# First expert layer with an unsplit fp32 w2: a second product in full fp32, and low halves of w1 on VectorE alone

## The chip, the cores and the metric

One core of a Trainium2 chip runs the whole program. The metric is device time of one execution in microseconds (us), of which the median of a few executions is taken. TensorE (PE) does matrix products and writes PSUM; VectorE (DVE), ScalarE (ACT) and GpSimd (POOL) do elementwise work; SyncE (SP) issues the plain transfers, GpSimd the indexed ones.

## The reference, cut to what matters

Attention comes first, with the query pooled in pairs; its output is a matrix `x` of 2304 tokens by 512. Two expert layers follow, each with eight experts of 512 x 1024 and 1024 x 512 weights. In the first, a token is computed only where its skip score is positive:

```python
for e in range(E):                       # first layer; second: the same with a further gate
    mask = e_idx == e
    h = np.maximum(xc[mask] @ w1[e], 0.0)
    y[mask] = gate_w[mask, None] * (h @ w2[e])
out[do_compute] = xc + y                 # x of the second layer
```

All data are float32.

## The kernel before

**Numbers.** TensorE takes an operand either as fp32 or as fp32r, a reduced form. A product near fp32 accuracy is built here of three fp32r products: each operand is split into a high half (a cast to fp32r) and a low half (what is left of it), and high x high, high x low and low x high are added in PSUM. So w1, w2, the tokens `x` and the hidden values `h` each have a high and a low tile (`w1h`/`w1l`, `w2h`/`w2l`, `xh`/`xl`, `hh`/`hl`).

**Weights.** Per expert, w1 and w2 come as 16 chunks of 256 KB (128 partitions x 512 values): chunks 0 to 7 are w1, 8 to 15 are w2. `load_w(s)` issues them on SP into a ring `raw` of 15 chunks; chunk c waits for the landing of chunk c - 4 (`DEPTH`) and for its ring slot, that is, for the split of the chunk that held it. `split(s, c)` makes the halves: the high one on ScalarE (line 188), the low one, a subtraction (line 190), on GpSimd for the chunks in the lists below (in most units of the first layer seven of sixteen, four of them in w1) and else on VectorE. Weight tiles exist twice, for even and odd s.

```python
POOL_P0 = (1, 3)                              # first unit of the first layer
POOL_LO = (1, 3, 5, 7, 10, 12, 14)            # its other units
POOL_L2 = (5, 7, 9, 11, 13, 15)               # second layer
```

**Units.** Tokens are listed by expert in a table, and a unit works on 256 or 128 of them with one expert's weights. Each layer begins with one unit P (256 tokens, of the fullest expert); then for each of the eight experts there is a unit F (128 tokens), and, behind branches that depend on the counts, units D (256 tokens more) and at most one S (128 tokens more). A block of 128 tokens has one second product, so P and D have two blocks, F and S one. In this data the first layer runs P, eight F (called F0 to F7 here), two D, behind F2, and one S, behind F5: 15 blocks. The order is P, F0 to F2, D, D, F3 to F5, S, F6, F7.

**Inside F and S** (`gemm1_S`, `gemm2`): 24 products of w1 (line 815), a copy of the result and its transposes (819, 824), ReLU with split (206, 207), then 24 products of w2 in two halves (834) with the transposes of the next tokens between them (198). The split of the next expert's weights (unit F and P alone) is spread over the unit, w1 within the first product, w2 after it.

**Routing for the second layer** (`route2`) rides along in each first-layer unit for the block finished before: transposes of its output (857), logits (868, 882), then a chain of small VectorE operations from line 884 to 892 that ends in `ohs`, which products on lines 901 to 905 read. Those stand in TensorE's order between the transposes on line 824 and the second product.

**Order.** Each engine runs its instructions in order; the ends of the units F are branches (lines 1068 and 1069). All of SP's loads for unit s + 2 are issued at the end of unit s. GpSimd issues the gather of the next tokens, the scatter of results and the table's records at the head of each unit.

**Around it.** The weights of P are loaded and split during the last of 16 head pairs of the attention, two chunks per step j; four of P's eight w1 groups run amid the attention's last work.

Of the kernel before, what the change touches and what calls it, by code (L numbers as in the profile page):

```python
# [25 lines left out]
F = 1024  # L26
# [10 lines left out]
BIG = 65536.0  # L37
EPS = 1e-9
DEPTH = 4
RING = 15  # L40
# [75 lines left out]
def build(ctx, tc, kT, qT, vt, wg, wa1, wa2, cst, out):  # L116
# [26 lines left out]
    ident = C("ident")  # L143

    def load_w(s):
        if s >= 18:
            return
        m, j = divmod(s, 9)
        e = j - 1 if j else nc.sync.value_load(eP[0:1, m:m + 1], min_val=0, max_val=7)
        w = (wa1, wa2)[m][ds(e, 1)].rearrange("o p (c f) -> (o p) c f", f=512)  # L150
        ins = []

        def chunk(c):
            i = nc.sync.dma_start(raw[:, (16 * s + c) % RING, :], w[:, c, :])
            if c >= DEPTH:
                tc.add_manual_dep(i.ins, ins[c - DEPTH].ins.name,
                                  mybir.DependencyInfo(mybir.DependencyClass.Sync, mybir.DependencyReason.DATA),
                                  reason="few loads in flight")
            ins.append(i)

        for c in range(RING):
            chunk(c)
        rest[s] = chunk

    def behind(i, js):
# [6 lines left out]

    def split(s, c, pool=POOL_LO, dve=(), after=()):
        if s >= 18:
            return
        i = s % 2
        r = raw[:, (16 * s + c) % RING, :]
# [12 lines left out]
        behind(eng.tensor_tensor(l, r, h.bitcast(F32), ALU.subtract), after)  # L190
        if c < 16 - RING:
            rest[s](RING + c)
# [11 lines left out]

    def relu_split(ps, hi, lo):
# [3 lines left out]
    def gemm1_D(i, post, cs_=range(8), banks=None):  # L209
        for c in cs_:  # L210
            o = (banks or pH)[c % 3][:, :256]
            cc = slice(c * P, (c + 1) * P)
            n = 0
            for k in range(4):
                for w, x in ((w1h[i], xh), (w1h[i], xl), (w1l[i], xh)):
                    nc.tensor.matmul(o, w[:, k, cc], x[:, k, :], start=(n == 0), stop=(n == 11))  # L216
                    n += 1
            relu_split(o, hh[c // 4][:, c % 4, :], hl[c // 4][:, c % 4, :])
            post(c)
# [5 lines left out]
    rest = {}  # L225
    w1h, w1l, w2h, w2l, hh, hl = ([None] * 2 for _ in range(6))
    with ExitStack() as es_:
# [402 lines left out]
        for p in range(NP):  # L630
# [8 lines left out]
            for j in range(KT):  # L639
# [65 lines left out]
                if p == NP - 1 and j == 0:  # L705
# [6 lines left out]
                    w1h[0], w1l[0] = (mp.tile([P, 4, F], F32R, name=n) for n in ("w1h0", "w1l0"))  # L712
                    w2h[0], w2l[0] = (mp.tile([P, 8, 512], F32R, name=n) for n in ("w2h0", "w2l0"))
# [3 lines left out]
                    hh[0], hl[0] = (mp.tile([P, 4, 2 * P], F32R, name=n) for n in ("hh0", "hl0"))  # L717
                    load_w(0)
                if p == NP - 1:
# [13 lines left out]
        def early_chunk(c):  # L733
            if c < NP0:
                gemm1_D(0, lambda c: None, (c,), (pH[0], pX[0], pX[1]))

# [27 lines left out]
    t72 = mp.tile([1, 8, 9], F32, name="t72")  # L764
    hh[1], hl[1] = (mp.tile([P, 4, 2 * P], F32R, name=n) for n in ("hh1", "hl1"))
    xc, yo = (mp.tile([P, 2, DM], F32, name=n) for n in ("xc", "yo"))
# [39 lines left out]

    def gemm1_S(i, hook):
        hq = (ht, xc[:, 0, :])
# [12 lines left out]
        for f in range(2):  # L821
            o = pH[2 - 2 * f]
            for k in range(4):
                nc.tensor.transpose(o[:, k * P:(k + 1) * P], hq[f][:, k * P:(k + 1) * P], ident)  # L824
            relu_split(o.rearrange("p (k c) -> p k c", c=P), hh[f][:, :, :P], hl[f][:, :, :P])
            hook(5 + f)

    def gemm2(i, o, h, fs):
# [103 lines left out]
    def unit(m, kind, e, pos, urgent=(), ahead=None):  # L932
# [36 lines left out]
        def pre(*cs):  # L969
            if kind in "FP":  # L970
                for c in cs:
                    split(s + 1, c, POOL_P0 if first else POOL_LO if not m else POOL_L2, DVE_F[m], urgent if e == 0 else ())

# [4 lines left out]
        if kind == "D":  # L978
            steps = {0: head, R2D[0]: lambda: r2(0), R2D[1]: lambda: r2(1), R2D[2]: lambda: r2(2)}
            gemm1_D(i, lambda c: steps[c]() if c in steps else None)  # L980
            gemm2(i, 0, 0, (0, 1))
            half()
            r2(3)
            xprep()
            gemm2(i, 1, 1, (0,))
            if m == 0:
                turn(0)
            if ahead:
                ahead()
            gemm2(i, 1, 1, (1,))  # L990
            return
        if kind == "P":
# [21 lines left out]
            if first:  # L1014
                head()
            gemm1_D(i, post, range(NP0 if first else 0, 8))
            pre(*range(8, PB[m]))
            gemm2(i, 0, 0, (0, 1))
            half()
            pre(*range(PB[m], 16))  # L1020
            load_w(s + 2)
            gemm2(i, 1, 1, (0,))
            if m == 0:
                turn(0)
            j = gemm2(i, 1, 1, (1,))
# [10 lines left out]

        gemm1_S(i, hook)
        j = gemm2(i, 1, 0, (0,))
# [6 lines left out]
        gemm2(i, 1, 0, (1,))  # L1045

# [5 lines left out]

    for m in range(2):
        x = unit(m, "P", -1, 0)
        codes = []
# [58 lines left out]
```

## Time and profile before

| | |
|---|---|
| median of 3 executions | 1203.73 us (1199.67 to 1214.24) |
| profiled execution, whole | 1207.56 us |
| its span, first to last instruction | 1205.9 us |
| mean granted TensorE clock | 0.948 |
| busy: PE, DVE, ACT, POOL | 1057.7, 843.0, 604.1, 432.6 us |
| attention | up to 563 us |
| first expert layer, end of P to start of the second layer | 599.46 to 860.14 us |

Busy time is the union of an engine's instructions; for PE the ends are modelled, and a PE that waits at half clock counts as busy. The profiled execution is 3.8 us above the median. What a change in the first layer does is to be read from the units between 599 and 860 us.

### The profile page before, as it was taken

The page shows a single profiled execution, that of the slowest core. Times are in us where ns is not written, and L with a number is a line of the kernel's source. Part 1 is how long each engine was busy: PE and PEld are TensorE (multiplying, and loading weights), DVE is VectorE, ACT ScalarE, POOL GpSimd, SP SyncE. Part 2 cuts the span into 40 slices and gives each one's busy share as a digit, 9 for nine tenths or more (in the row PEclk, how much of TensorE's full clock was granted, in tenths as well). Part 3 has the DMA queues.
Part 4 walks back from the last instruction along what each step waited for, and adds up shares of the span by engine and source line. Part 5 has one row for each costly group of instructions (what it writes and reads, how often), then busy time and mean ns, then how long its engine had stood idle before and what let it go on. Part 6 is the DMA issues. An engine that isn't in the chain of part 4 may idle for free. (4 is left out here: it accounts for less than half of the span.)

```text
span 1205.9 us, 19802 instructions
## 1 busy us (share of the span) xinstructions
PE 1057.7 (88%) x6520; PEld 799.7 (66%) x6520; DVE 843.0 (70%) x1486; ACT 604.1 (50%) x1466; POOL 432.6 (36%) x481
## 2 busy tenths in 40 slices
PE   3899998999999998899876997778788898989987
PEld 2666665666666666565755885566676786879865
DVE  6789998899899989875777536767955335452252
ACT  3566665666656665455564325636544326241142
POOL 6222222322121223100565325656756236451252
PEclk9899999999999999899997998989898999999989
DMA  9644443334244432053376304545757246451010
GB/s 229 161 109 109 109 109 99 92 90 100 66 109 106 102 88 60 19 176 116 119 238 197 107 30 144 179 138 170 223 171 227 62 137 205 150 195 35 22 44 21
DMA packets 72955, 146.58 MB, mean 122 GB/s; under 512 B 12652, under 2 KB 21612, under 8 KB 72738
## 3 DMA queue, kind: packets, MB, share of 16 engines
q1 hardware_dynamic: 63330, 127.65, 37.1%
q0 software_dynamic: 9408, 16.48, 4.5%
q8 instruction: 82, 1.34, 0.5%
q14 instruction: 135, 1.11, 0.3%
HBM read 138.18 MB, written 15.05 MB: 127 GB/s over the span
## 5 line engine op out<-in xcount | busy, mean ns | idle before, releaser
L385 ACT ACTIVATE PT<-pS 128x288 f32<-128x288 f32 x576 | 206.5, 409 | 143.0 <-PE pS L384 141.3
L358 DVE TENSOR_REDUCE mx<-pA 128x1 f32<-128x1152 f32 x144 | 194.9, 1356 | 27.3 <-PE pA L353 20.1
L381 PE MATMUL pS<-QQ,KK 128*128 128x288 f32 x576 | 184.6, 334 | 19.5 <-ACT PT L385 19.1
L392 PE MATMUL pO<-PT,V 128*64 128x288 f32 x1152 | 182.5, 427 | 0.0
L384 PE MATMUL pS<-QM,KB 73*128 73x288 f32 x576 | 166.5, 300 | 0.0
L338 POOL TENSOR_TENSOR QM<-qs,QQ 64x576 fp32r<-64x576 f32 x32 | 48.4, 1513 | 315.8 <-ACT QQ L324 216.0
L381 PEld LDWEIGHTS pS<-QQ,KK 128*128 128x128 f32 x576 | 110.3, 192 | 71.5 <-ACT PT L385 29.8
L207 DVE SCALAR_TENSOR_TENSOR hl<-pH,hh 128x256 fp32r<-128x256 f32 (+1 forms) x114 | 57.6, 505 | 78.7 <-ACT hh L206 78.2
L384 PEld LDWEIGHTS pS<-QM,KB 73*128 73x128 f32 x576 | 111.3, 193 | 0.0
L392 PEld LDWEIGHTS pO<-PT,V 128*64 128x64 f32 x1152 | 72.7, 138 | 55.3 <-issue 27.6
L353 PE MATMUL pA<-KK,QQ 128*128 128x384 f32 x384 | 92.8, 352 | 18.3 <-DVE KK L308 9.7
L188 ACT CAST w1h<-raw 128x512 fp32r<-128x512 f32 x141 | 79.1, 620 | 50.3 <-PEq L1074 29.4
L206 ACT ACTIVATE hh<-pH 128x256 fp32r<-128x256 f32 (+1 forms) x114 | 51.5, 452 | 93.7 <-PE pH L216 78.5
L190 DVE TENSOR_TENSOR w1l<-raw,w1h 128x512 fp32r<-128x512 f32 x94 | 83.9, 925 | 18.3 <-ACT w1h L188 18.1
L834 PE MATMUL pY<-w2h,hl 128*128 128x512 f32 x304 | 86.9, 409 | 10.9 <-DVE hl L207 10.9
L834 PE MATMUL pY<-w2h,hh 128*128 128x512 f32 x304 | 96.2, 441 | 0.0
L405 DVE TENSOR_TENSOR acc<-acc,PT 128x576 f32<-128x576 f32 x128 | 94.9, 761 | 1.0
L190 POOL TENSOR_TENSOR w2l<-raw,w2h 128x512 fp32r<-128x512 f32 x56 | 80.4, 1449 | 41.6 <-ACT w2h L188 29.6
L815 PE MATMUL pH<-w1h,xh 128*128 128x512 f32 x144 | 65.8, 457 | 28.4 <-ACT w1h L188 11.4
L216 PE MATMUL pH<-xh,w1h 128*128 128x256 f32 x312 | 89.4, 287 | 1.2 <-DVE hl L207 0.9
L834 PE MATMUL pY<-w2l,hh 128*128 128x512 f32 x304 | 89.5, 418 | 0.0
L216 PE MATMUL pH<-xl,w1h 128*128 128x256 f32 x312 | 88.2, 283 | 1.1 <-DVE xl L202 1.1
(218 smaller groups left out, 2136.3 us busy)
## 6 DMA issues: line engine op xcount, KB each, us to landing
raw<-wa SPq DMA_DIRECT2D x288, 256.0 KB, 3.7
rawQ<-qT SPq DMA_DIRECT2D x64, 288.0 KB, 6.9
rawK<-kT SPq DMA_DIRECT2D x64, 288.0 KB, 4.5
V<-vt SPq DMA_DIRECT2D x16, 576.0 KB, 5.5
xb<-xr SPq DMA_DIRECT2D x14, 288.0 KB, 2.7
xg<-xb,idn POOLq DMA_INDIRECT x54, 3.6
xb<-xr POOLq DMA_DIRECT2D x2, 288.0 KB, 3.9
tab<-rec,pidx POOLq DMA_INDIRECT x24, 2.1
```

Of the source, the lines that this page charges most:

```text
L188: behind(nc.scalar.copy(h, r), after)
L190: behind(eng.tensor_tensor(l, r, h.bitcast(F32), ALU.subtract), after)
L216: nc.tensor.matmul(o, w[:, k, cc], x[:, k, :], start=(n == 0), stop=(n == 11))
L353: nc.tensor.matmul(o, QQ[h][i][:, u * P:(u + 1) * P], KK[h][i][:, cc], start=True, stop=True)
L358: i = nc.vector.tensor_reduce(mx[p % 2 if p or t < 5 else 1][:, t:t + 1], pA[:, :, :384], AX.XY, ALU.max)
L381: m = nc.tensor.matmul(o, KK[h][i][:, k], QQ[h][i][:, c], start=True, stop=False)
L384: nc.tensor.matmul(o, KB[h][p % 2][:64 + NB, k], QM[h][i][:64 + NB, c], start=False, stop=True)
L385: exps.append(nc.scalar.activation(PT[(p * KT + j) % 4][h][:, c], o, AF.Exp, scale=0.0625))
L392: i = nc.tensor.matmul(pO[f][64 * h:64 * h + 64, :HQ], V[p % 3][:, j, h, :], PT[(p * KT + j) % 4][h][:, c], start=(j == 0), stop=(j == KT ...
L405: nc.vector.tensor_tensor(a, a, t, ALU.add)
L815: nc.tensor.matmul(pH[f], x[:, k, :P], w[:, k, fc], start=(n == 0), stop=(n == 11))
L834: j = nc.tensor.matmul(pY[o], a[:, k, hc], w[:, 4 * f + k, :], start=(n == 0), stop=(n == 23))
```

## The change

In the first layer, w2 is loaded straight into an fp32 tile `w2r` (one for even, one for odd s) and used as it is; the hidden values are one fp32 tile `hr`, written by ScalarE's ReLU; `gemm2` is 8 fp32 products per block in place of 24 fp32r ones. There is no split of w2 and no `hl`. The ring holds w1 alone, so a load of eight chunks takes 8 slots of 15. `load_w2(s + 1)` is issued at the head of unit s, `load_w(s + 2)` at its end, as before. All low halves of w1 are made on VectorE. The second layer keeps its three fp32r products and `POOL_L2`; its w2 tiles take the place of `w2r` and `hr` after the first layer. F7 splits weights of the second layer and so uses `POOL_L2` in place of `POOL_LO`.

```diff
-POOL_P0 = (1, 3)
-POOL_LO = (1, 3, 5, 7, 10, 12, 14)
+NL = 9
+    def slot(s, c):
+        return (8 * s + c if s < NL else 8 * NL + 16 * (s - NL) + c) % RING
...
-        for c in range(RING):
+        for c in range(8 if s < NL else RING):
             chunk(c)
+    def load_w2(s):
+        if s >= NL:
+            return
+        w = source(s)
+        ins = []
+        for k in range(8):
+            few(nc.sync.dma_start(w2r[s % 2][:, k, :], w[:, 8 + k, :]), ins)
...
-    def split(s, c, pool=POOL_LO, dve=(), after=()):
-        if s >= 18:
+    def split(s, c, dve=(), after=()):
+        if s >= 2 * NL or (s < NL and c >= 8):
             return
...
-        eng = nc.gpsimd if c in pool else nc.vector
+        eng = nc.gpsimd if s >= NL and c in POOL_L2 else nc.vector
...
+    def relu_split(m, ps, f, k):
+        if m == 0:
+            nc.scalar.activation(hr[f][k], ps, AF.Relu)
+            return
...
+            if m == 0:
+                for k in range(4):
+                    j = nc.tensor.matmul(pY[o], hr[f][:, k, hc], w2r[i][:, 4 * f + k, :],
+                                         start=(f + k == 0), stop=(f * k == 3))
+                continue
...
-                    for c in range(2 * j, min(2 * j + 2, 16)):
-                        split(0, c, (), DVE_HI)
+                    if j < 8:
+                        split(0, j, DVE_HI)
...
             if n == 0:
                 head()
+                if kind == "F" and m == 0:
+                    load_w2(s + 1)
...
+        if m:
+            zero.close()
+            mo = pool(ctx, "mo")
+            w2h[0], w2l[0] = (mo.tile([P, 8, 512], F32R, name=n) for n in ("w2h0", "w2l0"))
+            hl[0], hl[1] = (mo.tile([P, 4, 2 * P], F32R, name=n) for n in ("hl0", "hl1"))
```

`few` is the old rule of four loads in flight, as a function of its own; the slots of w2 loads are not part of the ring.

## Rows read from the trace of the kernel before

**Rows 1.** Windows, F0 to F7: length, busy us (instructions), PEclk, DMA share, GB/s.
```profile
599.46:621.96 22.50, 17.26 (x83) 13.29 (x82) 17.51 (x37) 13.96 (x29) 12.55 (x11) 0.87 0.88 286
621.96:646.62 24.66, 16.97 (x86) 13.18 (x86) 19.26 (x38) 13.72 (x28) 15.41 (x17) 0.85 0.68 214
646.62:670.57 23.95, 18.69 (x85) 14.67 (x86) 19.45 (x38) 12.21 (x25) 17.98 (x23) 0.80 0.58 179
670.57:696.29 25.72, 25.72 (x178) 22.89 (x177) 9.11 (x36) 7.06 (x16) 6.88 (x11) 1.00 0.16 52
...
726.83:750.96 24.13, 19.04 (x86) 14.51 (x86) 17.76 (x37) 13.50 (x28) 13.47 (x12) 0.83 0.59 175
750.96:775.64 24.68, 18.23 (x86) 14.10 (x86) 19.31 (x38) 13.59 (x27) 15.48 (x18) 0.86 0.59 186
775.64:800.06 24.42, 18.25 (x86) 13.64 (x86) 19.09 (x38) 12.15 (x25) 15.66 (x18) 0.86 0.58 177
800.06:815.23 15.17, 15.04 (x86) 11.91 (x86) 6.75 (x29) 6.46 (x13) 8.54 (x17) 1.00 0.15 51
815.23:837.51 22.28, 16.53 (x86) 12.80 (x85) 18.22 (x38) 13.28 (x27) 12.74 (x11) 0.92 0.58 177
837.51:860.14 22.63, 18.07 (x86) 13.51 (x86) 19.01 (x39) 12.34 (x26) 15.84 (x18) 0.85 0.67 210
```

**Rows 2.** Waits of PE from 599.4 to 837.6 us: total, times, longest.
```profile
PE pR L901 <- DVE ohs L892: 25.9, 6, 5.3
PE pH L815 <- DVEq L1068: 6.1, 3, 2.5
...
PE pY L834 <- DVE hl L207: 4.1, 1, 4.1
PE pH L815 <- ACT w1h L188: 3.1, 2, 1.7
PE pH L815 <- DVEq L1069: 1.9, 1, 1.9
```

**Rows 3.** Timelines of DVE and POOL, units S and F6: start, length, instruction.
```profile
805.92 0.17 DVE L887 TENSOR_TENSOR sm<-lgs,s 128x16 f32<-128x16 f32 x1
...
821.26 4.42 DVE L887 TENSOR_TENSOR sm<-lgs,s 128x16 f32<-128x16 f32 x1
...
820.67 3.75 POOL L190 TENSOR_TENSOR w1l<-raw,w1h 128x512 fp32r<-128x512 f32 x3
```

**Rows 4.** Line 190 from 599.46 to 837.51 us: ns min/median/max.
```profile
L190 DVE TENSOR_TENSOR w1l<-raw,w1h x28: 678/691/6182, 600.5 to 825.8; 128x512 fp32r<-128x512 f32 x28
```

**Rows 5.** Timeline of PE, end of unit S: fp32r products.
```profile
814.30 1.09 PE L834 MATMUL pY<-w2h,hl 128*128 128x512 f32 x4
815.23 0.40 PE L815 MATMUL pH<-w1h,xh 128*128 128x512 f32 x1
```

**Rows 6.** Timelines of PE and its weight loads: fp32 products.
```profile
300.14 1.19 PE L392 MATMUL pO<-PT,V 128*64 128x288 f32 x8
301.26 0.40 PE L381 MATMUL pS<-QQ,KK 128*128 128x288 f32 x1
...
704.02 0.64 PE L868 MATMUL pR<-x2T,wgs 128*32 128x256 f32 x8
...
706.01 0.53 PEld L882 LDWEIGHTS pR<-cs,x2T 128*128 128x128 f32 x4
```

**Rows 7.** Timeline of SP: loads of weight chunks issued one behind another.
```profile
594.11 27.33 SPq L154 DMA_DIRECT2D raw<-wa  x29
```

**Rows 8.** Timelines of DVE and PE, end of unit P.
```profile
590.54 5.30 DVE L190 TENSOR_TENSOR w2l<-raw,w2h 128x512 fp32r<-128x512 f32 x6
...
596.56 0.66 PE L857 MATMUL pX<-cs,yo 128*128 128x128 f32 x4 [2.35 <-DVE yo L841]
```

**Rows 9.** Last head pair, 530 to 563 us: casts of w2, waits of weight loads.
```profile
L188 ACT CAST w2h<-raw x7: 610/620/622, 544.8 to 555.4; 128x512 fp32r<-128x512 f32 x7
...
PEld pS L381 <- ACT PT L385: 4.8, 11, 0.4
```

More of the change, by code (lines that the diff above doesn't have):

```diff
@@ L143, in build, with source, few @@
     ident = C("ident")
+    def slot(s, c):
+        return (8 * s + c if s < NL else 8 * NL + 16 * (s - NL) + c) % RING
+    def source(s):
+        if s not in src_of:
+            m, j = divmod(s, NL)
+            e = j - 1 if j else nc.sync.value_load(eP[0:1, m:m + 1], min_val=0, max_val=7)
+            src_of[s] = (wa1, wa2)[m][ds(e, 1)].rearrange("o p (c f) -> (o p) c f", f=512)
+        return src_of[s]
+    def few(i, ins):
+        if len(ins) >= DEPTH:
+            tc.add_manual_dep(i.ins, ins[-DEPTH].ins.name,
+                              mybir.DependencyInfo(mybir.DependencyClass.Sync, mybir.DependencyReason.DATA),
+                              reason="few loads in flight")
+        ins.append(i)
     def load_w(s):
-        if s >= 18:
+        if s >= 2 * NL:
             return
-        m, j = divmod(s, 9)
-        e = j - 1 if j else nc.sync.value_load(eP[0:1, m:m + 1], min_val=0, max_val=7)
-        w = (wa1, wa2)[m][ds(e, 1)].rearrange("o p (c f) -> (o p) c f", f=512)
+        w = source(s)
         ins = []
         def chunk(c):
[L154 to L159, printed above, removed]
-        for c in range(RING):
+            few(nc.sync.dma_start(raw[:, slot(s, c), :], w[:, c, :]), ins)
+        for c in range(8 if s < NL else RING):
             chunk(c)
         rest[s] = chunk
+    def load_w2(s):
+        if s >= NL:
+            return
+        w = source(s)
+        ins = []
+        for k in range(8):
+            few(nc.sync.dma_start(w2r[s % 2][:, k, :], w[:, 8 + k, :]), ins)
     def behind(i, js):
@@ L171, in behind @@
         return i
-    def split(s, c, pool=POOL_LO, dve=(), after=()):
-        if s >= 18:
+    def split(s, c, dve=(), after=()):
+        if s >= 2 * NL or (s < NL and c >= 8):
             return
         i = s % 2
-        r = raw[:, (16 * s + c) % RING, :]
+        r = raw[:, slot(s, c), :]
         if c < 8:
@@ L225, in build @@
     rest = {}
-    w1h, w1l, w2h, w2l, hh, hl = ([None] * 2 for _ in range(6))
+    src_of = {}
+    zero = ExitStack()
+    w1h, w1l, w2h, w2l, hh, hl, w2r, hr = ([None] * 2 for _ in range(8))
     with ExitStack() as es_:
@@ L716, in build @@
                     pH = [pp.tile([P, 512], F32, name="pH0")]
-                    hh[0], hl[0] = (mp.tile([P, 4, 2 * P], F32R, name=n) for n in ("hh0", "hl0"))
+                    mz = pool(zero, "mz")
+                    for i in range(2):
+                        w2r[i] = mz.tile([P, 8, 512], F32, name=f"w2r{i}")
+                        hr[i] = mz.tile([P, 4, 2 * P], F32, name=f"hr{i}")
                     load_w(0)
+                    load_w2(0)
                 if p == NP - 1:
-                    for c in range(2 * j, min(2 * j + 2, 16)):
-                        split(0, c, (), DVE_HI)
+                    if j < 8:
+                        split(0, j, DVE_HI)
                     if j == JX:
@@ L764, in build @@
     t72 = mp.tile([1, 8, 9], F32, name="t72")
-    hh[1], hl[1] = (mp.tile([P, 4, 2 * P], F32R, name=n) for n in ("hh1", "hl1"))
+    hh[0], hh[1] = (mp.tile([P, 4, 2 * P], F32R, name=n) for n in ("hh0", "hh1"))
     xc, yo = (mp.tile([P, 2, DM], F32, name=n) for n in ("xc", "yo"))
@@ L971, in pre @@
                 for c in cs:
-                    split(s + 1, c, POOL_P0 if first else POOL_LO if not m else POOL_L2, DVE_F[m], urgent if e == 0 else ())
+                    split(s + 1, c, DVE_F[m], urgent if e == 0 else ())
         def half():
@@ L1015, in unit @@
                 head()
-            gemm1_D(i, post, range(NP0 if first else 0, 8))
+                load_w2(1)
+            gemm1_D(m, i, post, range(NP0 if first else 0, 8))
             pre(*range(8, PB[m]))
-            gemm2(i, 0, 0, (0, 1))
+            gemm2(m, i, 0, 0, (0, 1))
             half()
@@ L1035, in hook @@
                     r2(c)
-        gemm1_S(i, hook)
-        j = gemm2(i, 1, 0, (0,))
+        gemm1_S(m, i, hook)
+        j = gemm2(m, i, 1, 0, (0,))
         r2(3)
```

32 lines of the change are left out of this document (16 added, 16 removed).

## The prediction

> **What bounds the kernel now.** The page's shares of busy time say little: TensorE is at 88% of the whole span, but that is a mean over an attention stage and two expert layers with limits of their own. So I cut the first layer into its units (windows) and asked what each costs. S and F do the same TensorE work (86 instructions each), but S, which splits no weights, takes 15.17 us at a granted clock of 1.00 (2.4 GHz), and the seven F0 to F6 take 22.3 to 24.7 us, 166.6 together, at a mean clock of 0.80 to 0.92, which means stretches at 1.2 GHz among those at 2.4 [rows 1]. Seven times S would be 106.2. Where are the other 60.4 us? The waits of TensorE give most of it: six times it waits for `ohs`, 25.9 us in all, once for `hl`, 4.1, together 30.0; at the ends of units, behind the branches, it waits 6.1 + 3.1 + 1.9 = 11.1 [rows 2]. What is left, 19.3 us, is work done at 1.2 GHz: the granted clock falls after such waits, and S, which has none, stays at 1.00 [rows 1].
>
> Why does `ohs` come late? The timelines of VectorE and GpSimd side by side: in S the operation of line 887 takes 0.17 us; in F6 the same one takes 4.42, beginning just after a run of three subtractions on GpSimd that lasts 3.75, and ending with it [rows 3]. VectorE is held by GpSimd's run, then everything queued behind, `ohs` among it, is late, and TensorE stands. The hold has nothing to do with line 887; it takes whatever VectorE operation meets the run: among the 28 low halves of w1 that VectorE makes in these units, of 0.69 us each, one took 6.18 [rows 4].
>
> **The change part by part.**
>
> *GpSimd's subtractions go (F0 to F6: seven per unit).* With them goes what held VectorE. Of the 30.0 us I leave 3, about 0.4 per unit, since VectorE takes four more low halves of w1: 4 x 0.69 = 2.8 us per unit [rows 4]. If all four stood ahead of `ohs` that would be 2.8 of delay; most will fit in VectorE's idle time before line 884, as in S it has only 6.75 us of work in 15.17 [rows 1]. Bounds 0 and 2.8 per unit, and 0.4 is near the row that has no low halves (S, no wait). On the other side it loses five low halves of w2 and two `hl`, so its queue is shorter after the first product. Gain 27 us (10 to 30).
>
> *The clock.* 19.3 us came from stretches at 1.2 GHz. The pauses at the branches stay and may still cool TensorE; I leave 4. Gain 15 (8 to 19).
>
> *Pauses at the branches.* They end on a signal from VectorE's branch in four cases of six and on a cast in two [rows 2]. VectorE will be done earlier against TensorE, because its backlog of w2 is gone and the second half of the second product gets longer. I take 11.1 to 7, gain 4 (0 to 9).
>
> *The second product in fp32.* Before, four fp32r products of 512 columns go by in 815.23 - 814.30 = 0.93 us, 0.233 each at clock 1.00 [rows 5], so a block costs 24 x 0.233 = 5.6 us. No 128 x 512 product in fp32 stands in this trace. What stands there: each fp32 product in the program makes two records in the trace (four calls on line 868 make eight [rows 6]). The eight attention records of 288 columns take 301.26 - 300.14 = 1.12 us; two heads use half of the array each, side by side, so a pair takes 0.28, where 288 columns at 2.4 GHz are 0.12: 2.33 times [rows 6]. On line 868 four records run side by side on 32 columns each, 256 columns are 0.107 us at 2.4 GHz, and the eight records take 0.64 with the drain of the last, so the second four begin some 0.2 after the first: again two streams of the columns per record. For 512 columns a record then costs at least 2 x 512/2.4 = 0.427 us, at the fp32r rate per stream 0.467, at the attention's ratio 0.498. Sixteen records: 6.83, 7.47 or 7.97. I take 7.3, between the first two, because the fp32r row is the one with the same tile. That is 1.7 us more per block (1.2 to 2.35). Weight loads are no limit: four fp32 ones of 128 columns take 0.53 in all [rows 6], well under one record. F0 to F6: 7 x 1.7 = +12 (8 to 16).
>
> On the number of streams two pages of the Trainium skill differ. FP8 and Floating Point Precision, "TensorE Precision Notes", counts four passes for true fp32; the rows agree, with two records of two streams. Perfetto Trace Analysis, "Engine Utilization", has only a halved rate for the mode that it calls FP32_LOW_HIGH; if that meant two passes for the whole product, the second product would get cheaper and not dearer.
>
> Together F0 to F6: -27 - 15 - 4 + 12 = **-34**.
>
> *F7* (22.63 us [rows 1]) still splits w1 and w2 for the second layer with GpSimd, so its holds stay possible, but `hl` is gone as a victim. It has 7.5 us over S; I take half of that away and add 1.7: **-2** (-6 to +2).
>
> *The two units D* are TensorE's alone (busy 25.72 of 25.72 us, clock 1.00 [rows 1]). Nothing hides the four dearer blocks: 4 x 1.7 = **+7** (5 to 9). *S*, the same: **+2**.
>
> *P and the step to F0.* Two dearer blocks: +3.4. But at its end VectorE works through six low halves of w2 in a row, 5.30 us, ahead of the output of P's first block, and TensorE waits 2.35 for it, from 594.2 to 596.56 [rows 8]; F0's first product begins at 599.46 [rows 1], so 5.3 us lie between the units. Without those halves the output is long done and the chain shrinks to transposes and a cast, some 2 us. I call it even: **0** (-2 to +3).
>
> *The last head pair.* Seven casts of w2 of 0.62 us leave ScalarE there (VectorE made the eighth), and TensorE's weight loads wait 4.8 us for its exponentials, in 11 bits [rows 9]. **-1.5** (0 to -4).
>
> *The loads.* Same bytes, other order. Before, SP often stood for a ring slot; now a unit F issues eight w2 and eight w1 chunks that wait only for each other. 29 loads in a row took 27.33 us, 0.96 apart [rows 7], so 16 take 15.5, under the (166.6 - 34)/7 = 18.9 us of the new F. They are needed a unit later, so their landing is off the path at nothing, until a unit gets shorter than its loads.
>
> **Sum.** -34 - 2 + 7 + 2 + 0 - 1.5 = -28.5, say -29. Against its own execution: 1207.6 - 29 = 1178.6. That one lay 3.8 above the median; the change is worth the same from there: 1203.7 - 29.5 = **1174 us**, 2.5% less. Two per cent (1179.7) is about what a measurement of this kernel tells from no change.
>
> **The rivals.**
>
> *The loads become the bound.* Each F moves 4.2 MB of weights and its gathers and scatters; in F0, with loads dense, the DMA share was 0.88 [rows 1]. At 1.3 us per chunk, a third over rows 7, 16 take 20.8, 1.9 more than my F; over seven units +13: 1187. For it: the high share; against it: 0.96 in rows 7, with gathers beside them. Chance 0.12.
>
> *fp32 at the dear end*, 0.498 per record: +0.65 x 15 blocks = +10: 1184. For it: the attention's ratio is the only one measured on a stream of plain fp32. Chance 0.10.
>
> *Slower: the hold is traded for a queue.* VectorE works in order. If all eight low halves, each waiting for ScalarE's cast, are put ahead of lines 884 to 892, `ohs` stays as late as it is and TensorE waits and cools as before. Then the 27 + 15 + 4 do not come and the price stays: +12 + 7 + 2 - 1.5 - 2 = +17.5: 1221. The whole change pays only while more than about 40% of the 46 us (2.5 of 6.6 us per F) comes back. Against it: in S, where GpSimd subtracts nothing, the chain's operation is 0.17 long [rows 3], and a low half is 0.69, not 4 [rows 4]. Chance 0.06.
>
> *Everything goes* (no waits left, no pauses, no cold clock): 14 more: 1160. For it: S, which has none of them [rows 1]. Chance 0.15.
>
> *Two passes for fp32*: a record at 0.233, 16 x 0.233 = 3.7 per block, -1.9 in place of +1.7, 15 x 3.6 = 54 less: 1120. Lines 392 and 868 speak against it [rows 6]. Chance 0.03. The page on trace analysis named above is what could be read so.
>
> **How the numbers follow.** The forecast has 0.54 (1168 to 1182). The range takes in the dear fp32, the loads and the best case and leaves out 1221 and 1120: 1160 to 1189. Faster by over 2%: most of the forecast (0.48), the best case and the two passes, 0.66. Slower by over 2% needs the queue and the dear fp32 together: 0.02. The rest, 0.32, is within.
>
> **What would show it.** Units F0 to F6 at about 19 us and a clock near 0.95; no GpSimd subtraction before F7, and no VectorE operation of 0.17 us that takes 4; waits on line 901 of about 3 us in all; fp32 records of the second product 0.43 to 0.47 apart, D at 29, S at 17. I am wrong if line 901 still waits 4 us a unit, if fp32 records stand 0.5 or more apart, or if SP's loads end last in a unit and TensorE waits for casts of chunks that have not landed.

## The result, and the profile after

The changed kernel took **1170.22 us** (median of four executions, 1168.41 to 1175.5) against 1203.92 (1199.67 to 1214.24) for the kernel before: ratio **0.9708**, 95% interval 0.9646 to 0.9769. The profiled execution took 1175.5 us, its span 1173.8, at a mean granted clock of 0.97. That is the longest of the four, and the run "after again" below says what that is worth. Ratios and intervals, here and below, come from executions in the fast state alone and are not the quotients of the medians shown.

In the changed kernel's line numbers the first product of a unit F or S is line 842 and that of a unit D 237; the second product, now fp32, is 860, the subtraction 207, the cast 205, the chain's operations 919 to 926 (`ohs` on 924), the products that read `ohs` 933 and 937, the branches 1108 and 1109, and the loads 168 (`raw`) and 180 (`w2r`).

The windows of the units after, in their order (F0, F1, F2, both D, S, F6, F7 are shown; length, busy us of PE, PEld, DVE, ACT, POOL, then PEclk, DMA share, GB/s), answer to [rows 1]:

```profile
599.09:616.72 17.63, 16.43 (x78) 9.97 (x76) 9.83 (x33) 9.13 (x19) 3.35 (x3) 1.00 0.71 236
616.72:636.38 19.66, 16.93 (x77) 10.13 (x78) 10.08 (x35) 9.89 (x21) 7.25 (x11) 1.00 0.77 246
636.38:653.13 16.75, 16.22 (x78) 10.30 (x78) 10.09 (x35) 8.48 (x18) 8.18 (x12) 1.00 0.86 284
653.13:681.48 28.35, 28.35 (x163) 20.02 (x162) 6.03 (x28) 7.06 (x16) 7.48 (x15) 1.00 0.09 30
681.48:712.21 30.73, 28.91 (x164) 19.99 (x162) 6.04 (x28) 7.95 (x18) 5.07 (x5) 1.00 0.09 29
...
766.66:782.77 16.11, 15.97 (x78) 10.22 (x78) 5.61 (x27) 6.40 (x13) 8.52 (x17) 1.00 0.35 103
782.77:800.69 17.92, 16.89 (x80) 10.28 (x78) 13.49 (x35) 12.32 (x26) 7.37 (x6) 1.00 0.53 170
800.69:820.35 19.66, 17.18 (x78) 10.08 (x78) 12.62 (x38) 9.12 (x19) 9.60 (x13) 1.00 0.60 193
```

Read the clock first: it is 1.00 in every unit, where F0 to F7 had 0.80 to 0.92. F0 to F6 take 126.4 us together (F3 17.72, F4 18.48) instead of 166.6, which is 40.2 less. Units D, which are TensorE's alone, are longer, the first by 2.63. VectorE's busy time in a unit F0 to F5 is 9.8 to 10.1 us, against 17.5 to 19.5 before. The second layer begins at 820.35 instead of 860.14.

TensorE's waits over F0 to F6 (total, times, longest), against [rows 2]:

```profile
PE pH L842 <- ACT w1h L205: 4.3, 4, 1.8
PE pX L215 <- DMA xg<-xb,idn: 2.5, 3, 1.5
PE pH L851 <- issue: 1.2, 5, 0.2
PE pH L842 <- PEq L1109: 1.0, 1, 1.0
PE pH L842 <- ACTq L1108: 1.0, 1, 1.0
PE pH L842 <- PEq L1108: 0.8, 1, 0.8
```

No wait for `ohs` and none for `hl` is left, out of 30.0 us. Line 842 still waits at the ends of units, 4.3 + 1.0 + 1.0 + 0.8 = 7.1, but no longer for VectorE's branch. One wait is new: the transposes of the next tokens (line 215) wait 2.5 us for their gather. On VectorE the chain is short again (timeline in F5: start, length), as it was in S in [rows 3]:

```profile
755.88 0.17 DVE L919 TENSOR_TENSOR sm<-lgs,s 128x16 f32<-128x16 f32 x1
755.97 0.68 DVE L207 TENSOR_TENSOR w1l<-raw,w1h 128x512 fp32r<-128x512 f32 x1
...
757.18 0.18 DVE L924 TENSOR_TENSOR ohs<-sm,s 128x16 bf16<-128x16 f32 x1
```

The "queue on VectorE" is there too, and it is short: three low halves of 0.68 us stand among the chain's operations in F5 (from 754.60, 755.28 and 755.97), so the chain from its first copy (754.46) to the end of `ohs` takes 2.90 us, where it took 1.46 in S before. That this costs TensorE nothing has another reason: the order of TensorE's instructions is not the same in the two kernels, although no line of the change asks for it. Before (unit F4), all products that read `ohs` stand behind the first four transposes of line 824, ahead of everything else:

```profile
759.87 0.60 PE L824 MATMUL pH<-cs,ht 128*128 128x128 f32 x4
765.52 0.19 PE L901 MATMUL pR<-ohs,upb 128*128 128x8 bf16 x2 [5.06 <-DVE ohs L892]
```

After (unit F5), one of them stands behind all eight transposes (now line 851; the last of them begin at 756.96), and the others only behind the first half of the second product:

```profile
756.12 0.60 PE L851 MATMUL pH<-cs,ht 128*128 128x128 f32 x4
...
757.45 0.17 PE L933 MATMUL pR<-ohs,upb 128*128 128x8 bf16 x1
757.51 3.67 PE L860 MATMUL pY<-w2r,hr 128*128 128x512 f32 x8
...
761.05 0.17 PE L935 MATMUL pR<-ohs,onb 128*128 128x8 bf16 x1
```

F1 to F6 are all like this; in F0 all of them stand behind the first half, and S and F7 have the old order. In each of F0 to F6, `ohs` is ready 0.77 to 0.86 us after the place where the old order would have needed it (the end of the first four transposes). So at most 5.5 us of the 25.9 in [rows 2] are hidden by the new order; the rest of them is gone.

TensorE's timeline in S shows the price of the fp32 product:

```profile
775.32 3.70 PE L860 MATMUL pY<-w2r,hr 128*128 128x512 f32 x8
778.86 1.04 PE L215 MATMUL pX<-cs,xg 128*128 128x128 f32 x8
779.73 3.60 PE L860 MATMUL pY<-w2r,hr 128*128 128x512 f32 x8
782.77 0.80 PE L842 MATMUL pH<-w1h,xh 128*128 128x512 f32 x1
783.40 0.39 PE L842 MATMUL pH<-w1l,xh 128*128 128x512 f32 x1
```

Four products make eight records. From the first to what follows them are 778.86 - 775.32 = 3.54 us, in which the first record has an extra 0.1; so a record takes (3.54 - 0.1)/8 = 0.43, and a block 16 x 0.43 = 6.9, where 24 fp32r products took 5.6 [rows 5]: 1.3 us more. The window of S is only 0.94 longer than before, because it ends at the recorded start of F6's first product, 782.77. By then the last of the eight records, begun at 779.73 + 7 x 0.43 = 782.74, has hardly started, and F6's second product follows the first by 0.63 and not by 0.23. Counted with these 0.4, S is 1.3 longer as well.

### The profile page after: what moved, and what is told of

It is laid out like the page before. It is cut to its first block, busy times and chain, and to the rows that moved or that the text cites. A ratio compares the mean times of both kernels' runs of the same rounds, so it can differ in the third digit from the quotient of the medians.

```text
span 1173.8 us, 19240 instructions
## 1 busy us (share of the span) xinstructions
PE 1056.1 (90%) x6400; PEld 762.3 (65%) x6400; DVE 764.5 (65%) x1423; ACT 567.9 (48%) x1395; POOL 362.2 (31%) x429
## 5 line engine op out<-in xcount | busy, mean ns | idle before, releaser
L382 DVE TENSOR_REDUCE mx<-pA 128x1 f32<-128x1152 f32 x144 | 194.9, 1356 | 32.5 <-PE pA L377 20.3
L860 PE MATMUL pY<-w2r,hr 128*128 128x512 f32 x240 | 108.1, 596 | 0.4 <-issue 0.4
L207 DVE TENSOR_TENSOR w1l<-raw,w1h 128x512 fp32r<-128x512 f32 x126 | 88.7, 743 | 12.3 <-ACT w1h L205 11.2
L218 ACT CAST xh<-pX 128x512 fp32r<-128x512 f32 x56 | 30.9, 589 | 128.5 <-PE pX L215 101.8
L237 PE MATMUL pH<-xh,w1l 128*128 128x256 f32 x312 | 88.4, 284 | 0.0
L842 PE MATMUL pH<-w1h,xh 128*128 128x512 f32 x144 | 62.1, 431 | 22.6 <-ACT w1h L205 13.9
L377 PEld LDWEIGHTS pA<-KK,QQ 128*128 128x128 f32 x384 | 67.3, 200 | 22.3 <-DVE mx L382 11.7
L228 DVE SCALAR_TENSOR_TENSOR hl<-pH,hh 128x256 fp32r<-128x256 f32 (+1 forms) x74 | 36.0, 486 | 61.3 <-ACT hh L227 58.5
L860 PEld LDWEIGHTS pY<-w2r,hr 128*128 128x128 f32 x240 | 43.5, 190 | 46.0 <-issue 42.5
```

The lines of the kernel that those rows point to most:

```text
L377: nc.tensor.matmul(o, QQ[h][i][:, u * P:(u + 1) * P], KK[h][i][:, cc], start=True, stop=True)
L382: i = nc.vector.tensor_reduce(mx[p % 2 if p or t < 5 else 1][:, t:t + 1], pA[:, :, :384], AX.XY, ALU.max)
L842: nc.tensor.matmul(pH[f], x[:, k, :P], w[:, k, fc], start=(n == 0), stop=(n == 11))
L860: j = nc.tensor.matmul(pY[o], hr[f][:, k, hc], w2r[i][:, 4 * f + k, :], start=(f + k == 0), stop=(f * k == 3))
```

## The experiments

Nine further kernels were run, two of them twice, and the changed kernel once more. "Seven F" is the sum of F0 to F6 in the profiled execution; "holds" are TensorE's waits for `ohs` and `hl` by name in those units. Medians stand beside the kernel before on the same chip, at 1201.5 to 1205.8. The first layer's order of TensorE's products is the old one in "before", in "w1 low halves back on GpSimd" and in "before, with gaps", and a later place for the products that read `ohs` in all others.

| kernel | median us | ratio, 95% interval | seven F | holds |
|---|---|---|---|---|
| before | 1203.92 | | 166.6 | 30.0 |
| after | 1170.22 | 0.9708 (0.9646 to 0.9769) | 126.4 | 0 |
| after again | 1163.50 | 0.9704 (0.9653 to 0.9755) | 125.7 | 0 |
| before, low halves on VectorE | 1171.94 | 0.9756 (0.9720 to 0.9792) | 134.7 | 0 |
| after, w1 low halves back on GpSimd | 1207.90 | 1.0065 (1.0024 to 1.0105) | 158.6 | 14.3 |
| after, w2 loaded twice only | 1159.57 | 0.9672 (0.9634 to 0.9710) | 123.9 | 0 |
| after, GpSimd fills | 1173.68 | 0.9782 (0.9723 to 0.9842) | 125.7 | 0 |
| after, subtractions repeated | 1192.61 | 0.9916 (0.9875 to 0.9956) | 149.9 | 9.3 |
| the same without gaps | 1212.06 | 1.0055 (1.0026 to 1.0084) | 174.5 | 25.6 |
| before, with gaps | 1202.61 | 0.9979 (0.9941 to 1.0017) | 158.9 | 17.7 |
| before, both layers on VectorE | 1155.27, 1154.36 | 0.9627 (0.9584 to 0.9671), 0.9564 (0.9529 to 0.9600) | 133.3, 136.2 | 0 |
| after, both layers on VectorE | 1145.55, 1144.43 | 0.9532 (0.9496 to 0.9567), 0.9498 (0.9461 to 0.9535) | 127.6, 127.2 | 0 |

### One half of the change: low halves off GpSimd

```diff
-POOL_P0 = (1, 3)
+POOL_P0 = ()
-POOL_LO = (1, 3, 5, 7, 10, 12, 14)
+POOL_LO = ()
```

> The kernel before, with one part of the change alone: every low half of the first layer (w1 and w2) is made on VectorE; w2 is still split, the second product still takes 24 fp32r products. Theory 1 (GpSimd's subtractions held VectorE, and that cost the waits and the slow clock): the waits for ohs and hl in F0 to F6, 30 us, and most of the 19 us at 1.2 GHz go although VectorE gets seven more low halves of 0.69 us a unit; F0 to F6 near 18.5 us each, 1163 to 1178 us in all. Rival (the gain came from work taken off VectorE and ScalarE): VectorE has 17 operations of 0.69 us a unit in place of 10, F0 to F6 stay at 24 us or grow, 1204 to 1225 us.

The kernel before with this edit gives 1171.94 us, ratio 0.9756. w2 is still split and the second product is still fp32r, so VectorE has sixteen low halves per unit and not eight. All the same there is no wait for `ohs` or `hl`. What is left, in TensorE's waits over F0 to F6:

```profile
PE pH L815 <- DVEq L1068: 12.4, 4, 4.7
PE pH L815 <- DVE yo L841: 3.9, 1, 3.9
PE pH L815 <- DVEq L1069: 3.6, 1, 3.6
```

and the window of one of its units, F1:

```profile
622.40:642.20 19.80, 16.62 (x86) 12.54 (x86) 14.94 (x45) 13.84 (x28) 7.47 (x11) 0.93 0.71 230
```

Of the 40.2 us that the seven units gave back, 166.6 - 134.7 = 31.9 come with this edit. But TensorE's order changed with it here as well. TensorE's and VectorE's timelines in F4:

```profile
740.41 0.60 PE L824 MATMUL pH<-cs,ht 128*128 128x128 f32 x4
...
743.73 1.10 PE L834 MATMUL pY<-w2h,hl 128*128 128x512 f32 x4
744.67 0.21 PE L901 MATMUL pR<-ohs,upb 128*128 128x8 bf16 x2
...
742.96 0.17 DVE L892 TENSOR_TENSOR ohs<-sm,s 128x16 bf16<-128x16 f32 x1
```

The products that read `ohs` stand behind the first half of the second product in all seven units. `ohs` is ready at 743.13, and the transposes are through at 740.85: in the old order TensorE would have stood 2.3 us here, and at most 16.8 in the seven units (2.3 to 3.0 each). That lateness isn't GpSimd's; it is VectorE's own queue, with low halves of w1 and w2 and `hl` among the chain's operations. So the 31.9 us are the hold and the order together, and no run has these low halves in the old order. That the hold alone costs as much is shown by three kernels further down, which all have the changed kernel's order.

The second thing to see is what comes late next: at the branches TensorE waits 16.0 us for VectorE (8.0 in [rows 2]), which has 13.9 to 15.0 us of work in a unit. So the unsplit w2 pays too, in another place: it takes eight low halves out of VectorE's unit. The 16.0 us at the ends of the units F become 5.3, the granted clock, 0.86 to 1.00 in the seven units here, becomes 1.00, and the dearer product takes some of it back: 134.7 to 126.4, 8.3 us. From F0 to the second layer it is less (226.8 to 221.3), as the two D pay the price too, and the intervals of the two ratios overlap.

### The other half alone: w2 unsplit, GpSimd kept

```diff
-        eng = nc.gpsimd if s >= NL and c in POOL_L2 else nc.vector
+        back = (1, 3) if s == 1 else (1, 3, 5, 7) if s else ()
+        eng = nc.gpsimd if c in (POOL_L2 if s >= NL else back) else nc.vector
```

> The changed kernel with the low halves of w1 chunks 1, 3, 5 and 7 back on GpSimd in the first layer (1 and 3 in unit P); w2 stays unsplit and the product fp32. Theory 1: runs of four subtractions on GpSimd hold VectorE for 4 to 5 us a unit again, F0 to F6 near 23 us, 1195 to 1207 us. Rival: VectorE loses four operations of 0.69 us a unit, so nothing is lost: 1165 to 1173 us.

1207.90 us, 0.9 over what I had expected, ratio 1.0065: without GpSimd's part the unsplit w2 gains nothing on the whole, and the interval lies above 1. TensorE's order is the old one here. The seven units are 8.0 us shorter than before, but the two D, S and F7 (28.35, 30.82, 16.08 and 27.56 us) are 8.7 longer, 4.9 of them in F7, which comes back under the fills. The seven are 17.64, 25.84, 22.82, 17.75, 25.74, 24.22 and 24.56 us long. Why two of them are as short as after can be read from VectorE's and GpSimd's timelines, in F0 and in F5:

```profile
607.41 5.58 DVE L952 TENSOR_SCALAR s<-s 128x2 f32<-128x2 f32 x1
...
775.23 5.63 DVE L925 TENSOR_TENSOR ohs<-sm,s 128x16 bf16<-128x16 f32 x1
...
775.90 4.92 POOL L208 TENSOR_TENSOR w1l<-raw,w1h 128x512 fp32r<-128x512 f32 x4
```

Each unit has one hold, of 4.4 to 5.7 us, which ends with GpSimd's run (775.23 + 5.63 = 780.86; 775.90 + 4.92 = 780.82). It began 0.67 us ahead of the run's first record; what GpSimd does in that time isn't in the trace. In F0 it falls on line 952, behind `ohs`, and costs nothing; in F5 it falls on `ohs`, and TensorE stands. The list of TensorE's waits over F0 to F6 has two names for it:

```profile
PE pR L934 <- DVE ohs L925: 14.3, 3, 5.2
PE pY L861 <- ACT hr L225: 10.9, 2, 5.5
```

The second is the same hold seen through ScalarE: in F1 it fell just behind `ohs`; ScalarE's next operation (line 929) waited 5.43 us for its result, and `hr`, queued behind it, was late for the second product.

### The loads

```diff
-        if s >= NL:
+        if s >= 2:
```

> The changed kernel without the loads of w2 after the first two units of the first layer (later units multiply by the w2 that lies there, so the first layer's result is another). Theory 1: the loads are off the path, 16 of them take 15.5 us of a unit of 18; F0 to F6 and the total unchanged within 4 us, 1166 to 1174 us. Rival (the transfers set the pace of the new F): units F shrink to 16.5 us or less, 1158 us or less.

With half the bytes the seven units take 123.9 us instead of 126.4, and S the same 16.1. So the loads are off the path, but for 2.5 us in seven units at most. The whole time, 1159.57, lies 6 us under the range that I had given, and says little, since the second layer works on other counts here. In the changed kernel SP's timeline shows what the prediction had worked out, 16 loads in 15.6 us:

```profile
616.04 6.33 SPq L180 DMA_DIRECT2D w2r<-wa  x8
622.42 9.26 SPq L168 DMA_DIRECT2D raw<-wa  x8
```

### Is it the read, and how long does it hold?

Three kernels put work back on GpSimd that nobody needs, in the changed kernel, for chunks 1, 3, 5 and 7 of w1. The first fills a scratch tile; the second repeats the subtraction into one; the third does the same into a scratch slot for each chunk.

```diff
+        if 1 < s < NL and c in (1, 3, 5, 7):
+            more = nc.gpsimd.memset(w2l[1][:, 0:5, :256].bitcast(F32), 0.0)      # first, behind the cast
+            nc.gpsimd.tensor_tensor(w2l[1][:, 0, :]..., r, h, ALU.subtract)      # second
+            nc.gpsimd.tensor_tensor(w2l[1][:, c, :]..., r, h, ALU.subtract)      # third
```

> The changed kernel; in F0 to F6, GpSimd also fills a scratch tile four times (128 x 1280 values each, after the casts of chunks 1, 3, 5 and 7), which reads nothing; VectorE's work is unchanged. Theory 1 in the narrow form (what holds VectorE is GpSimd reading operands): no hold, 1166 to 1173 us. In the wide form (any busy GpSimd holds it): a run of four fills, some 4.8 us, holds VectorE in most units, 1190 us or more.

> The changed kernel; in F0 to F6, GpSimd makes the low halves of chunks 1, 3, 5 and 7 a second time into a scratch tile (28 subtractions that nobody reads), while VectorE makes all eight as in the changed kernel. Theory 1: VectorE is held for a run of four, 4 to 5.5 us, in most units, with a colder clock behind: 1190 to 1210 us. Rival (with those four on GpSimd the time came from waiting for their result, not from a hold): nothing waits for the scratch, 1166 to 1174 us.

> The changed kernel with GpSimd repeating the low halves of w1 chunks 1, 3, 5 and 7 in the units F0 to F6, as in the run of doubled subtractions, but each into a scratch tile of its own, so that GpSimd's four instructions no longer wait for each other's output. There they stood 0.04 us apart, and four operations of VectorE's chain were held for 1.1 to 1.6 us each; in the kernel before, GpSimd's instructions overlapped by 0.05 us and one operation was held 4.42. Theory: the hold ends only where GpSimd leaves a gap. Then here one operation of VectorE per unit is held for what is left of the run, 3 to 5.5 us, and none or few are held for one instruction alone. Rival: the hold is for one instruction at a time, and the long one of the kernel before came from something else: then again several of 1.1 to 1.6 us. The time by the theory 1190 to 1205, as the chain has at least four operations with two inputs in a row and loses about the run either way, and what stands between them is now late as well; by the rival as before, 1187 to 1198.

**Fills**: the seven units take 125.7 us, as after again. GpSimd is nearly as long at it as with subtractions (four fills of 1.2 us a unit, 4.86 in all), and VectorE's operations with two inputs run through beside it, 0.16 and 0.17 us for two of them, in GpSimd's and VectorE's timelines of F5:

```profile
751.65 4.86 POOL L209 MEMSET w2l<- 128x1280 f32 x4
...
753.00 1.08 DVE L956 TENSOR_SCALAR s<-s 128x2 f32<-128x2 f32 x1 [1.10 <-ACT s L933]
754.12 0.16 DVE L957 SCALAR_TENSOR_TENSOR s<-s,s 128x2 f32<-128x2 f32 x1
...
756.27 0.17 DVE L948 TENSOR_TENSOR sm<-prs,ohs 128x16 f32<-128x16 f32 x1
```

What is held is the fp32 TENSOR_SCALAR with one input, 0.34 to 1.12 us in place of 0.17, and by less a CAST of 2 values per partition (0.40 to 0.50); both stand behind `ohs` and cost nothing. The units' time alone would prove little: in six of the seven units `ohs` begins 0.33 to 0.40 us before the first fill, and only in F6 does the chain itself run beside the fills (all its operations at their usual length). But in the run without gaps below, an operation that began 0.3 to 0.6 us before GpSimd's first subtraction was held through its whole run. So neither GpSimd's time nor its place in the order held the chain.

The whole time, 1173.68, is still 10 us above "after again", and outside those units: F7, which has no fill, took 28.62 us there, against 19.7 after, with a wait of 4.0 for `ohs`. VectorE's and GpSimd's timelines in F7:

```profile
806.09 4.93 DVE L207 TENSOR_TENSOR w1l<-raw,w1h 128x512 fp32r<-128x512 f32 x1
...
806.76 2.49 POOL L207 TENSOR_TENSOR w1l<-raw,w1h 128x512 fp32r<-128x512 f32 x2
```

A third subtraction follows until 810.46. This is the same hold, by GpSimd's usual subtractions for the second layer, on a low half ahead of `ohs`, and in F7 TensorE has the old order. After, after again and in the run without gaps, the hold of F7 fell on a TENSOR_SCALAR behind `ohs`, and F7 took 19.7 to 20.5 us; with w1's low halves back on GpSimd and with repeated subtractions it fell ahead of `ohs`, 27.6 us. So some 8 us of the changed kernel hang on where this one run falls. What shifts it isn't settled.

**Repeated subtractions**: nobody reads what they write, and the units take 149.9 us. VectorE's timeline in F3, beside GpSimd's run of four from 723.15 to 728.92:

```profile
722.85 1.63 DVE L921 TENSOR_TENSOR sm<-lgs,s 128x16 f32<-128x16 f32 x1
...
725.01 1.24 DVE L922 SCALAR_TENSOR_TENSOR sm<-sm,cs 128x16 f32<-128x16 f32 x1
...
726.48 1.10 DVE L925 TENSOR_TENSOR sm<-sm,s 128x16 f32<-128x16 f32 x1
727.62 0.17 DVE L926 TENSOR_TENSOR ohs<-sm,s 128x16 bf16<-128x16 f32 x1
```

Here the hold isn't one of 4 to 6 us but three or four of 0.9 to 1.9. The four subtractions write the same scratch slot, so each waits for the one before, and they stand 0.08 us apart; in the kernel before, each in a run began 0.03 to 0.07 us before the end of the last. **Without gaps**, with the same instructions in the same order on every engine and only the slots different, there is one long hold in each of the seven units (5.27 to 5.54 us), as in F3:

```profile
738.85 5.54 DVE L925 TENSOR_TENSOR sm<-sm,s 128x16 f32<-128x16 f32 x1
744.42 0.17 DVE L926 TENSOR_TENSOR ohs<-sm,s 128x16 bf16<-128x16 f32 x1
...
739.43 4.92 POOL L209 TENSOR_TENSOR w2l<-raw,w1h 128x512 fp32r<-128x512 f32 x4
```

The waits for `ohs` are 25.6 us instead of 9.3, the seven units 174.5 instead of 149.9 (and F7 20.45 instead of 27.60), and the time 1212.06 instead of 1192.61: 20 us for gaps of some hundredths of a microsecond. The holds came as the theory had them; the time lies 7 us above my range. All three kernels have the changed kernel's order on TensorE, so against its 126.4 us the subtractions alone cost 23.5 with gaps and 48.1 without, and the fills nothing.

### Gaps in the kernel before

```diff
+        low = behind(eng.tensor_tensor(l, r, h.bitcast(F32), ALU.subtract), after)
+        if s < 9 and c in pool:
+            if s in gap:       # a semaphore wait for GpSimd's last subtraction of this expert
+                tc.add_manual_dep(low.ins, gap[s].ins.name, ...Sync...)
+            gap[s] = low
```

> The kernel before, with nothing moved: each low half that GpSimd makes in the first layer waits on a semaphore for the one that it made before for the same expert, so that its instructions stand a few hundredths of a microsecond apart and no longer overlap. Theory, from the two runs with doubled subtractions, which issue the same instructions in the same order and differ by 20 us: most of what GpSimd costs the units F0 to F6 comes from holds over whole runs. Then no operation of VectorE takes over 2 us there, the waits for ohs and hl fall from 30 to 8 to 14 us, the seven units from 166.6 to 145 to 153, and the time to 1182 to 1192, ratio 0.980 to 0.990. Rival: the chain loses the same to several short holds as to one long one: 1198 to 1208. Both would be wrong if the waits on the semaphore made GpSimd the late one for TensorE's low halves: over 1208.

1202.61 us, ratio 0.9979 (0.9941 to 1.0017): a miss. The first steps came as expected: no hold over 2 us, and 12.4 + 5.3 = 17.7 us for `ohs` and `hl` instead of 30.0. What was saved came back at the branches, in TensorE's waits over the same units:

```profile
PE pH L823 <- DVEq L1076: 14.2, 4, 4.5
PE pR L909 <- DVE ohs L900: 12.4, 6, 2.6
PE pH L823 <- DVEq L1077: 6.1, 1, 6.1
PE pY L842 <- DVE hl L215: 5.3, 4, 1.6
```

20.3 us for VectorE's branches (8.0 in [rows 2]). VectorE has 16.4 to 18.9 us of busy time in a unit here, held time included, and once the chain is earlier, its end is what TensorE meets. The seven units still gained 7.7 us, but the first D gave half of it back (29.60 instead of 25.72, at a clock of 0.94), and S and F7 the rest (2.7 and 1.2 more). So the gaps were worth 20 us in the changed kernel and nothing here. It fits that VectorE has less room here (13.4 to 14.5 us of work in F0 to F5 with repeated subtractions after the change), but TensorE's order is another too, and no run separates the two.

### The second layer, and a version that beats both

```diff
-POOL_L2 = (5, 7, 9, 11, 13, 15)
+POOL_L2 = ()
```

> The changed kernel with the second layer's low halves on VectorE alone as well (F7's split too); the second layer still splits w2 and takes three fp32r products. Theory 1: the second layer's waits for hl and ohs (11 us after the change) and the slow clock behind them go, VectorE has about 17 us of work in a unit F of 19: 1152 to 1165 us. Rival: VectorE becomes the bound of the second layer's F units: 1172 to 1185 us.

> The kernel before with every low half of both layers on VectorE; w2 split and three fp32r products in both. Theory 1 (GpSimd's subtractions are what cost): the same further gain as the changed kernel had from it in the second layer, some 25 us under the first-layer version (1172): 1143 to 1152 us, within 6 us of the changed kernel with the same edit (1146). Rival (the second layer's gain there came with the fp32 tiles' other memory and load order): 1165 us or more.

> The changed kernel with the low halves of the second layer on VectorE too, once more, to stand on one chip beside the kernel before with all low halves on VectorE. 1141 to 1150, ratio 0.950 to 0.957.

> The kernel before, with w2 still split, and all low halves of both layers on VectorE, on the same chip. If the unsplit w2 is worth something of its own once GpSimd splits nothing, this stays above the run beside it: I expect 1153 to 1160, 0.8 to 1.2% more. By TensorE alone it should be less: its fifteen blocks in fp32r are 1.3 us each, about 20 together, cheaper than in fp32. If the difference between the chips made the earlier one, the two come out within 4 us of each other.

The changed kernel with this line took 1145.55 us and, on another chip, 1144.43, 1.5 to 2% under the change itself, and the first 6 us under the range given for it: the second layer still splits w2 with GpSimd's help, and TensorE's waits there for `hl` and `ohs` (8.7 and 2.5 us in the first profile of after) are gone. The kernel before with all low halves on VectorE took 1155.27 and 1154.36; the first is 3 us above what I had expected. On the same chip the two stand 9.9 us apart, and their intervals, 0.9461 to 0.9535 and 0.9529 to 0.9600, hardly meet; no execution of one lies within those of the other. In the two profiles 7.4 us of it lie between F0 and the second layer (227.2 and 219.8), and the second layers are equal (325.7 and 325.6). So with GpSimd out of both layers the unsplit w2 is worth some 10 us, although its products are dearer.

### After, once more

> The changed kernel once more, beside the next one on the same chip, to size what is left of the change beyond the low halves. If w2 unsplit and the fp32 product are worth what the windows say (F0 to F6 134.7 us with all low halves on VectorE and w2 split, 126.4 with the change; D and S dearer by 2.6 each and 1), they give 2 to 8 us: 1164 to 1172 us here.

1163.50 us (1159.62 to 1169.47), ratio 0.9704, and a profiled span of 1158.2. Its first layer is like the other's (seven F 125.7, D 28.35). The second layer is not: from its start to the end of the span it took 353.4 us in the first profile (1173.8 - 820.35), 341.4 here (1158.2 - 816.79), and 345.8 before (1205.9 - 860.14). The 7.7 us by which the second layer seemed to grow are not a price of the change; its code is the same. The waits for `hl` tell one part: 8.7 us in three waits in the first profile, 2.8 before, none over 0.8 in this one. Ahead of it in VectorE's queue stand low halves of w2 that GpSimd's runs hold, the two longest for 7.33 and 7.40 us in the first profile and for 4.88 and 5.44 in this one. The same code meets the runs differently from one execution to the next.

## Why the prediction was right

Forecast 1174, measured 1170.22. The mechanism was the one predicted; that the number came so close is in part luck, as the last lines say. By its own steps:

- **The hold, and who causes it: right.** The three kernels with repeated subtractions and with fills carry it: at the same order on TensorE, subtractions that nobody reads bring the waits and the low clock back, and fills of the same length don't. One row was misread: [rows 3] shows GpSimd's run in F6 as three of 3.75 us because the view ends at 824. It is a run of four, 4.97 us, to 825.64, and the held operation ends at 825.68. And two of the 28 low halves were held, not one (6.18 and 5.52 us). The Trainium skill ("SBUF — State Buffer", section "Who interferes with whom") says that a VectorE instruction with two SBUF inputs contends with a GpSimd instruction that reads SBUF and not with one that only writes it, and that one in a 2-port mode contends with GpSimd; the runs agree with the first, 5.5 us beside subtractions and 0.18 beside fills. The 1.08 for the TENSOR_SCALAR beside a fill would fit the second, but no trace shows an instruction's mode. What the same section says of the length, that the pair is held for the whole instruction, was short of the trace here: where GpSimd's instructions overlap, one operation was held to the end of a run of four.
- **The waits: 27 of 30.0 us forecast, all 30.0 gone, in part for a reason that the prediction had not.** It took TensorE's order as given and left 3 us for the low halves on VectorE. They make `ohs` late by more, 0.77 to 0.86 us a unit, at most 5.5 in all, and the new order hides it. In the kernel with all of the first layer's low halves on VectorE it is 16.8: there the rival of the queue came true, and only the order kept it off the path.
- **The clock: right in kind, too small.** 15 of 19.3 us were to come back; the granted clock is 1.00 in every unit, so all did. It had been a result of the waits: it is back at 0.86 to 0.92 in five of the seven units with the repeated subtractions.
- **Pauses at the ends: a gain of 5.8 for 4, and of another kind.** Of the 7.1 us on line 842, 1.8 stand behind the second D, where before TensorE waited for `yo`, which isn't in the 11.1; behind units F 11.1 became 5.3. They no longer end on VectorE's branch but on the cast of w1 and on the branches of ScalarE and TensorE. That VectorE's backlog of w2 would have become the bound (16.0 us in the run with low halves on VectorE) is what the unsplit w2 avoids. The prediction named the backlog but gave it 4 us.
- **The fp32 product: right in sign and mechanism, mis-sized.** This is the term that was furthest off where it could be read directly. I took 1.7 per block, 0.456 per record, between the floor of 0.427 and the fp32r rate per stream of 0.467. The records are 0.43 apart and a block costs 1.3 more, as the first D shows for two blocks (+2.63). Choosing the middle was the mistake: the floor had been worked out from two rows [rows 6] that agreed on two streams per record. FP8 and Floating Point Precision of the Trainium skill, "TensorE Precision Notes", counts four passes for fp32; two records of two streams each agree, and the rival of two passes is out.
- **F0 to F6: -34 forecast, -40.2 measured.** By terms: the waits -30.0 for -27, the clock -19.3 for -15, the pauses -5.8 for -4, the product 7 x 1.3 = +9.1 for +12. That makes -46.0. Some 5.8 us came in that had no term: 2.5 are the wait for the gather and 1.7 small waits on line 851.
- **D: +7 forecast, +2.8 measured** (2.63 and 0.2). The price is 5.2 in all; what took half of it back is a row that I had not counted. Behind the second D, TensorE waited 4.7 us for `yo` on VectorE, and after the change 1.8 for a cast. **S** +1.3 (0.94 by its window) for +2, **F7** -3.0 for -2, with its hold fallen behind `ohs`, and the start of F0 -0.4 for -1.5 (-3.3 in the second profile: the 2.35 us of [rows 8] are down to waits of 0.6 in all, but when the attention ends varies by as much). One sign was off: three of GpSimd's subtractions for the second layer stand in F6 already, behind `ohs`.
- **The loads: right.** 16 in 15.6 us, forecast 15.5; off the path but for the 2.5 us above and the gather's 2.5.

The forecast for the first layer was -28.5 and its profile shows -39.8. That the median still came out 4 us from the forecast owes something to the second layer, and is luck to that extent: in the first profile it was 7.7 us longer than before, and in the second 4.4 shorter. By the second profile alone the execution was 1159.9, just below the range. Of the rivals, the best case (1160, no waits and no cold clock) came nearest within the first layer.

Open: how the gain of the first half divides between the hold and TensorE's order, what shifts the hold of F7 ahead of `ohs` or behind it, and which operations make VectorE late at the unit's end once GpSimd's instructions in the kernel before have gaps.

## What to carry to other kernels

Look on VectorE's timeline for a small operation that takes microseconds, and on GpSimd's for what ends with it; a GpSimd that "takes load off" VectorE with operations that read SBUF can cost more than it carries, and what counts is whether the hold falls ahead of or behind the operation that TensorE waits for. Before an engine is relieved, ask which engine comes late next: here GpSimd's half of the change, with the order that came with it, is worth 31.9 us in the seven units and the unsplit w2 8.3 behind it, and the unsplit w2 by itself nothing on the whole. When a wait goes, look at the waiting engine's order in both traces before you say why: an edit on one engine can move another engine's instructions. And where two rows give a floor for a price, take the floor unless a row speaks for more.

## What the runs showed of the hardware that was not expected

One VectorE operation of 0.17 us was held for a whole run of GpSimd subtractions (5.27 to 5.54 us for four) where these followed each other without a gap, and for one at a time (0.9 to 1.9 us) where a semaphore wait left 0.08 us between them. With the same instructions in the same order this made 1192.61 or 1212.06 us. A GpSimd fill, which reads nothing, held no operation with two inputs but did hold a TENSOR_SCALAR of 2 fp32 values per partition for up to 1.12 us.
